# Score rows fetched ten queries at a time into a fixed ring of ten slots, in an attention and gated feed-forward kernel

## The chip, the cores and the metric

The kernel runs on one core of one Trainium2 chip. The metric is the device time of one execution in microseconds (us); lower is better. Time before: 1014.11 us, median of 3 runs (1013.52 to 1015.11).

## What is computed

The inputs are float32: q, k, v of 4 batches x 12 heads x 448 rows x 64, two 12 x 12 matrices w_pre and w_post that mix heads, and the feed-forward weights of 768 x 2048 and 2048 x 768. The reference, cut to what matters:

```python
scores = scale * np.matmul(q, k.transpose(0, 1, 3, 2))
scores = np.einsum('bhij,hg->bgij', scores, w_pre)
scores = scores - np.max(scores, axis=-1, keepdims=True)
attn = np.exp(scores)
attn = attn / (np.sum(attn, axis=-1, keepdims=True) + 1e-09)
attn = np.einsum('bhij,hg->bgij', attn, w_post)
x = np.matmul(attn, v)          # heads side by side: 1792 x 768
h = x @ w_in
g = np.where(h >= 1, h, np.where(h <= -1, 0.0, (h + 1) ** 2 / 4.0))
out = g @ w_out
```

## The kernel before, in words

The program has two stages: attention, up to about 600 us, and the two feed-forward products after it. The change is in the first.

**Tiles and units.** A tile is 120 queries of one batch (the last of a batch has 88); there are 16. `scores` (lines 165 to 174) multiplies Q by K for all heads of a tile and `copy` puts the result into `ssb`, a buffer with the query on the partition and 12 heads x 448 keys along it. Mixing heads needs the heads on the partitions. So a tile is cut into units of 20 queries (the short tile has four and one of 8), and the rows of a unit are fetched from `ssb` into row tiles named `s`: one partition for each pair of query and head. Line 85 lists a unit's queries: two rows of ten queries each, a row's queries `np_` apart (6, in a short tile 4), and `k` = 2 says that a row is cut into two halves of five.

**Fetching** (`load_s`, lines 188 to 196). Each row tile takes two DMAs, one for the five queries of even rank (60 partitions, 0 to 59) and one for those of odd rank (64 to 123). They are issued on SyncE's queue (SP):

```python
for j in range(k):
    a = o + st * j
    nc.sync.dma_start(out=x[64 * j:64 * j + i * H], in_=ssb[t][a:a + st * k * (i - 1) + 1:st * k])
```

The row tiles come from a pool with ten buffers.

**Mixing and softmax.** `pre` (line 206) multiplies each half of a row tile by `wpre`, a block-diagonal matrix of five copies of w_pre, into PSUM (`ps_l`); the four products of a unit go to the four quarters of TensorE. `row_max` (L210, VectorE) finds the maxima, `exps` (L218, ScalarE) the exponentials, `norm` (L225 to L228, GpSimd and VectorE) the scaled copies `wr` of w_post, and `post` (L246) mixes the heads again and turns keys onto the partitions. `pv` (L270) multiplies by V.

**Order.** It is written out by hand: the loop at line 850 goes over 48 steps, each with a group of two units (the last group of a short tile has one). In step n the program places: `load_s` of the units of step n+1; `pre` of step n; `post` of the first unit of step n-1; transposes of a later tile's Q and, in some steps, K (L157, L141); `pv`; `scores` of two pairs of heads of a later tile; `post` of the other unit. In 32 of the steps a chunk of the feed-forward weights is loaded (`wraw`, L302, 768 KB), converted on ScalarE, VectorE and GpSimd, and stored to DRAM (L328, 384 KB); all of these DMAs are on SP's queue, behind `load_s`. Every DMA waits for the eighth DMA before it on that queue, since eight semaphores are used in turn (DMAHW0 to DMAHW7 in the rows of the order).

**Set-up.** GpSimd builds `ident` and one mask, loads the small matrices (L736), and issues four K loads (L738). VectorE makes `wpre` and `wpost` from mask and matrices (L771, L775).

Of the kernel before, what the change touches and what calls it, by code (L numbers as in the profile page):

```python
# [9 lines left out]
F32 = mybir.dt.float32  # L10
# [5 lines left out]
ALU = mybir.AluOpType  # L16
# [6 lines left out]
def tile_talking_heads_moe(  # L23
# [11 lines left out]
    nc = tc.nc  # L35
    B, H, S, D = q.shape
# [4 lines left out]
    IH = 5  # L41
    KH = IH * H
    QT = 24 * IH
    KC = 4
# [13 lines left out]
    ap_ = s_att.enter_context(tc.tile_pool(name="att", bufs=2))  # L58
# [17 lines left out]
    for b in range(B):  # L76
        for i0 in range(0, S, QT):
            t = len(tiles)
            n = min(QT, S - i0)
# [6 lines left out]
            if n > 4 * IH * np_:  # L86
                i = (n - 4 * IH * np_) // 2
# [11 lines left out]
    ssb = {}  # L99
# [6 lines left out]
    def pair(name):  # L106
        return ps_l.tile([128, 2, 512], F32, tag="l", name=name)

    def load_k(b, hp, t=None):
        es = {0: (nc.sync, nc.scalar), 1: (nc.sync, nc.scalar), 4: (nc.gpsimd,) * 2,  # L110
              5: (nc.gpsimd,) * 2}.get(hp if t is not None else None, (nc.sync,) * 2)
        w = 2 * KC * D
        if t is None:
            t = qp.tile([128, w], F32, tag="kraw", name="kraw", bufs=2)
            x = t[:KP]
        else:
            x = t[:KP, w * (hp % 2):w * (hp % 2 + 1)]
        x = x.rearrange("p (r s d) -> p r s d", s=2, d=D)
        for s in range(2):
            es[s].dma_start(out=x[:, :, s, :], in_=k[b, 2 * hp + s].rearrange("(p r) d -> p r d", r=KC))  # L120
        kraw[b, hp] = x

    def load_q(t, gs=(0, 1)):
        b, i0, n, nb = tiles[t]
        if 0 in gs:
            qraw[t] = qp.tile([128, H, D], F32, tag="qraw", name="qraw", bufs=2)
        for g in gs:
            h = slice(g * HP, (g + 1) * HP)
            nc.sync.dma_start(out=qraw[t][:n, h], in_=q[b, h, i0:i0 + n].rearrange("h p d -> p h d"))
# [46 lines left out]
    def copy(e, out, in_):  # L176
        if e is nc.vector:
            nc.vector.tensor_copy(out=out, in_=in_)  # L178
        else:
            nc.scalar.activation(out=out, in_=in_, func=AF.Copy)  # L180

    s10 = {}
    lps = {}
    ex = {}
    wr = {}
    aT = {}

    def load_s(m):
        t, rows, k, c = units[m]
        s10[m] = []  # L190
        for o, st, i in rows:
            x = ap_.tile([128, S], F32, tag="s10", name="s10", bufs=10)
            for j in range(k):
                a = o + st * j
                nc.sync.dma_start(out=x[64 * j:64 * j + i * H], in_=ssb[t][a:a + st * k * (i - 1) + 1:st * k])  # L195
            s10[m].append(x)

    def pre(m):
        t, rows, k, c = units[m]
        ps = lps[m] = pair("ps_l")  # L200
        xs = s10.pop(m)
        n = rows[0][2] * H
        for j in range(k):
            p = slice(64 * j, 64 * j + n)
            for x, h in zip(xs, half):
                nc.tensor.matmul(out=ps[h, j, :S], lhsT=wpre[p], rhs=x[p], start=True, stop=True)  # L206

# [27 lines left out]
    def post(m):  # L235
        t, rows, k, c = units[m]
        if t not in aT:
            aT[t] = ap_.tile([128, KC * H, QT], F32, tag="aT", name="aT")
        n = rows[0][2]
        ps = pair("ps_a")  # L240
        for j, (e, w) in enumerate(zip(ex.pop(m), wr.pop(m))):
            for r in range(KC):
                for x, p in enumerate((slice(0, KH), slice(64, 64 + KH))):
                    o = ps[:, x, :KC * KH * k].rearrange("p (r g i j) -> p r g i j", r=KC, g=H, j=k)
                    for y, h in enumerate((slice(0, 64), slice(64, KP))):
                        nc.tensor.matmul(out=o[h, r, :, :n, j], lhsT=e[p, r * KP + h.start:r * KP + h.stop],  # L246
                                         rhs=w[p].rearrange("p (g i) -> p g i", i=IH)[:, :, :n],
                                         start=True, stop=True)

        def out(e):  # L250
            z = n * k
            copy(e, aT[t][:KP, :, c:c + 2 * z].rearrange("p h (x i) -> p x h i", x=2),
                 ps[:KP, :, :KC * KH * k].rearrange("p x (h i) -> p x h i", h=KC * H)[:, :, :, :z])
        return out
# [450 lines left out]
    with tc.manual_schedule():  # L705
# [6 lines left out]
        ident = qp.tile([128, 128], F32, name="ident", bufs=1)  # L712
# [5 lines left out]
        for hp in (2, 3):  # L718
            load_k(0, hp, k0[1])
        load_q(1)  # L720
        wrep = ap_.tile([128, 4, KH], F32, tag="wr", name="wrep", bufs=2)
        wrep = wrep.rearrange("p a b -> p (a b)")[:, :2 * H].rearrange("p (n h) -> p n h", n=2)
        make_identity(nc, ident)
        nc.gpsimd.memset(wrep, 0.0)
        mask = ap_.tile([128, 4, KH], F32, tag="wr", name="mask", bufs=2)
        mask = mask.rearrange("p a b -> p (a b)")[:, :2 * IH].rearrange("p (n i) -> p n i", n=2)
        nc.gpsimd.memset(mask, 1.0)
        nc.gpsimd.affine_select(out=mask, in_=mask, compare_op=ALU.is_ge, fill=0.0,
                                base=0, pattern=[[-64, 2], [-H, IH]], channel_multiplier=1)
        nc.gpsimd.affine_select(out=mask, in_=mask, compare_op=ALU.is_ge, fill=0.0,  # L730
                                base=H - 1, pattern=[[64, 2], [H, IH]], channel_multiplier=-1)
        nc.gpsimd.tensor_tensor(out=mask[:, 0], in0=mask[:, 0], in1=mask[:, 1], op=ALU.add)
        mask = mask[:, 0]
        for n, w in enumerate((w_pre, w_post)):
            for p in range(2):
                nc.gpsimd.dma_start(out=wrep[64 * p:64 * p + KH, n, :], in_=w.unsqueeze(0).to_broadcast([IH, H, H]))  # L736
        for hp in (4, 5):
            load_k(0, hp, k0[2])  # L738

        ps_w = pair("ps_w")  # L740

# [24 lines left out]
        for m in groups[0]:  # L766
            load_s(m)
# [2 lines left out]
        nc.vector.memset(wpre, 0.0)  # L770
        nc.vector.scalar_tensor_tensor(  # L771
            out=wpre[:, :KH].rearrange("p (i g) -> p i g", g=H),
            in0=mask.unsqueeze(2).to_broadcast([128, IH, H]), scalar=float(D) ** -0.5,
            in1=wrep[:, 0, :].unsqueeze(1).to_broadcast([128, IH, H]), op0=ALU.mult, op1=ALU.mult)
        nc.vector.tensor_tensor(  # L775
            out=wpost.rearrange("p (g i) -> p g i", i=IH),
            in0=wrep[:, 1, :].unsqueeze(2).to_broadcast([128, H, IH]),
            in1=mask.unsqueeze(1).to_broadcast([128, H, IH]), op=ALU.mult)
        for hp in range(4):
            scored_now(1, hp)  # L780
        at = {}
# [68 lines left out]
        for n in range(NG + 2):  # L850
            if n == NE:
# [5 lines left out]
                    name="ps_h", bufs=1, space=PSUM, side="right", reuse_waits="tile"))  # L857
# [5 lines left out]
            if n + 1 < NG:  # L863
                for m in groups[n + 1]:
                    load_s(m)
# [5 lines left out]
            j = 0  # L871
            part = []
            for m in ms:
                pre(m)
                part.append(slice(j, j + units[m][2]))
                j += units[m][2]
            if n == NG:
                step(0)
            posted = [post(old.pop(0))] if old else []
            turned = [f() for f in at.pop(n, ())]  # L880
            for f in mid.pop(n, ()):
# [5 lines left out]
            if old:  # L887
                posted.append(post(old.pop(0)))
# [41 lines left out]
        for j in range(NJ):  # L930
            q, k = divmod(j, 7)
# [143 lines left out]
```

## Time and profile before

| | |
|---|---|
| median of 3 runs | 1014.11 us |
| the profiled execution | 1014.48 us |
| its span, first to last instruction | 1012.8 us |
| mean granted TensorE clock, share of full speed | 0.924 |
| TensorE (PE) busy | 922.1 us |
| VectorE, ScalarE, GpSimd busy | 614.1, 515.8, 108.0 us |
| row tile fetches, number and size | 352 of 105 KB, 8 of 84 KB |

The profile is of one execution, and its page cuts the span into 40 equal slices, so that a digit stands for 25 us. The page's list of costly instructions says for each line how long its engine sat idle just before it and what ended that; the chain follows the work that ended last back to its releasers. Matmuls that run on different quarters overlap, so the mean duration of one, times their number, is more than the busy time.

### The profile page before, as it was taken

What the parts mean: (1) busy time and instruction counts of PE and PEld (TensorE: products, weight loads), DVE (VectorE), ACT (ScalarE), POOL (GpSimd) and SP (SyncE); (2) the same over time, 40 slices, a digit from 0 to 9 for tenths busy, and PEclk for the clock granted to TensorE, in tenths of its full rate; (3) what the DMA queues carried; (4) which work ended last, traced back from release to release, by engine and by line L of the source; (5) the groups of instructions that cost most, each with busy time, mean ns of one, the idle gap of its engine ahead of it and who ended that gap; (6) DMA issues with size and microseconds to landing.
All of it is one profiled execution on the core that took longest, in us unless ns stands there. A gap on an engine that the chain in (4) does not pass through costs nothing.

```text
span 1012.8 us, 25676 instructions
## 1 busy us (share of the span) xinstructions
PE 922.1 (91%) x10986; PEld 716.8 (71%) x10986; DVE 614.1 (61%) x732; ACT 515.8 (51%) x932; POOL 108.0 (11%) x147
## 2 busy tenths in 40 slices
PE   8888898888898897898989689999999999999998
PEld 5455565454565454654656477888999999999998
DVE  4445455445554444554445388879966797867763
ACT  4536454545555445455446345666866754443331
POOL 2012102212112112022122020000000000000000
PEclk9879898889998778899779799999999999999999
DMA  7466566765556665566664637546444445313441
GB/s 148 148 180 175 160 157 176 208 194 160 168 151 188 202 198 160 149 178 197 195 196 153 186 106 244 191 165 230 156 128 135 150 140 176 122 48 95 124 139 57
DMA packets 148946, 162.84 MB, mean 161 GB/s; under 512 B 61132, under 2 KB 142432, under 8 KB 148832
## 3 DMA queue, kind: packets, MB, share of 16 engines
q1 hardware_dynamic: 147584, 160.49, 53.2%
q8 instruction: 87, 1.43, 0.6%
q0 software_dynamic: 320, 0.47, 0.3%
q10 hardware_dynamic: 928, 0.23, 0.1%
q14 instruction: 27, 0.22, 0.1%
HBM read 88.81 MB, written 33.82 MB: 121 GB/s over the span
## 4 chain that ended last, share of the span: by engine, by line
PE 58%; DMA 29%; SPq 7%; ACT 2%; DVE 2%; issue 1%; POOLq 1%; ACTq 0%; DVEq 0%
DMA s<-ssb 21%; PE ps_f L659 20%; PE ps_f L494 20%; PE ps_l L206 5%; PE ps_x L270 5%; PE ps_a L246 4%; SPq L195 4%; PE ps_s L172 3%; DMA wraw<-in_moe_w_out_dram 3%; ACT e L218 1%; DMA v<-in_v_dram 1%; DMA wsd<-wt 1%; DMA wraw<-in_moe_w_in_dram 1%; DMA k<-in_k_dram 1%; DVE nm L210 1%
## 5 line engine op out<-in xcount | busy, mean ns | idle before, releaser
L206 PE MATMUL ps_l<-s,wpre 60*64 60x448 f32 (+1 forms) x720 | 206.1, 598 | 54.3 <-DMA s<-ssb 50.6
L218 ACT ACTIVATE e<-ps_l,nm 128x448 f32<-128x448 f32 x180 | 112.3, 631 | 158.4 <-DVE nm L210 158.3
L206 PEld LDWEIGHTS ps_l<-s,wpre 60*64 60x64 f32 (+1 forms) x720 | 46.7, 137 | 169.4 <-DMA s<-ssb 130.1
L210 DVE TENSOR_REDUCE nm<-ps_l 128x2 f32<-128x896 f32 (+1 forms) x92 | 97.3, 1068 | 97.7 <-PE ps_l L206 97.2
L246 PEld LDWEIGHTS ps_a<-wr,e 60*64 60x64 f32 (+1 forms) x5760 | 122.7, 142 | 44.2 <-issue 30.3
L246 PE MATMUL ps_a<-wr,e 60*64 60x60 f32 (+2 forms) x5760 | 135.2, 237 | 8.8 <-ACT e L218 5.7
L270 PE MATMUL ps_x<-aT,v 112*64 112x120 f32 (+1 forms) x1408 | 98.4, 306 | 4.9 <-DVE kl L146 4.8
L642 ACT ACTIVATE sgh_p<-gq_p 128x1024 fp32r<-128x1024 f32 (+1 forms) x56 | 53.3, 953 | 90.1 <-PE ps_f L659 90.0
L659 PE MATMUL ps_f<-wh,sgh_p 128*128 128x384 f32 x294 | 98.2, 334 | 0.0
L659 PE MATMUL ps_f<-wh,sgl_p 128*128 128x384 f32 x294 | 98.2, 334 | 0.0
L659 PE MATMUL ps_f<-wl,sgh_p 128*128 128x384 f32 x294 | 98.2, 334 | 0.0
L178 DVE COPY ssb<-ps_s 120x896 f32<-120x896 f32 (+1 forms) x48 | 52.3, 1090 | 75.4 <-PE ps_s L172 71.6
L270 PEld LDWEIGHTS ps_x<-aT,v 112*64 112x64 f32 x1408 | 87.6, 166 | 11.8 <-DVE kl L146 6.9
L386 DVE SCALAR_TENSOR_TENSOR wl<-wi,wh 128x768 fp32r<-128x768 f32 x71 | 67.8, 954 | 41.9 <-ACT wh L383 41.9
L383 ACT ACTIVATE wh<-wi 128x768 fp32r<-128x768 f32 x71 | 59.7, 842 | 57.6 <-DVE wi L606 18.0
L643 DVE TENSOR_TENSOR sgl_p<-gq_p,sgh_p 128x1024 fp32r<-128x1024 f32 (+1 forms) x56 | 60.9, 1089 | 33.2 <-ACT sgh_p L642 33.2
L180 ACT ACTIVATE ssb<-ps_s 120x896 f32<-120x896 f32 (+1 forms) x48 | 44.0, 917 | 51.5 <-PE ps_s L172 50.3
L317 POOL TENSOR_TENSOR wt<-wt,wk 128x768 int32<-128x768 int32 x32 | 57.8, 1808 | 100.2 <-ACT wk L316 89.4
L178 DVE COPY aT<-ps_a 112x960 f32<-112x960 f32 x48 | 55.3, 1152 | 8.6 <-PE ps_a L246 8.5
L322 DVE TENSOR_SCALAR wt<-wt 128x768 int32<-128x768 int32 x32 | 17.9, 560 | 68.8 <-ACT wt L310 68.8
L659 PEld LDWEIGHTS ps_f<-wl,sgh_p 128*128 128x128 f32 x294 | 55.2, 188 | 0.0
L659 PEld LDWEIGHTS ps_f<-wh,sgh_p 128*128 128x128 f32 x294 | 55.2, 188 | 0.0
(209 smaller groups left out, 1661.3 us busy)
## 6 DMA issues: line engine op xcount, KB each, us to landing
s<-ssb SPq DMA_DIRECT2D x352, 105.0 KB
wraw<-in_moe_w_in_dram SPq DMA_DIRECT2D x16, 768.0 KB
wraw<-in_moe_w_out_dram SPq DMA_DIRECT2D x16, 768.0 KB
wi<-wod SPq DMA_DIRECT2D x29, 384.0 KB
wi<-wsd SPq DMA_DIRECT2D x28, 384.0 KB
wsd<-wt SPq DMA_DIRECT2D x16, 384.0 KB
wod<-wt SPq DMA_DIRECT2D x16, 384.0 KB
wi<-wss SPq DMA_DIRECT2D x16, 384.0 KB
```

Of the source, the lines that this page charges most:

```text
L178: nc.vector.tensor_copy(out=out, in_=in_)
L206: nc.tensor.matmul(out=ps[h, j, :S], lhsT=wpre[p], rhs=x[p], start=True, stop=True)
L210: nc.vector.tensor_reduce(out=nm, in_=lps[m][:, :k, :S], axis=AX.X, op=ALU.max, negate=True)
L218: nc.scalar.activation(out=e, in_=ps[:, j, :S], func=AF.Exp, bias=nm[:, j:j + 1], accum_out=sm[:, j:j + 1])
L246: nc.tensor.matmul(out=o[h, r, :, :n, j], lhsT=e[p, r * KP + h.start:r * KP + h.stop], rhs=w[p].rearrange("p (g i) -> p g i", i=IH)[:, :, :n],
L270: nc.tensor.matmul(out=ps[half[s], m, :n], lhsT=vt[b, g][:, 2 * m + s, r * D:(r + 1) * D], rhs=a[:KP, r * H + h, :n], start=(r == 0), stop ...
L317: nc.gpsimd.tensor_tensor(out=t, in0=t, in1=k, op=ALU.add)
L383: nc.scalar.activation(out=hi, in_=t, func=AF.Copy, scale=2.0 ** -8)
L386: nc.vector.scalar_tensor_tensor(out=lo, in0=t, scalar=2.0 ** -8, in1=hi.bitcast(F32), op0=ALU.mult, op1=ALU.subtract)
L494: nc.tensor.matmul(out=o, lhsT=u[:, c, k], rhs=x, start=first and r == 0 and m == 0, stop=r == 2 and m == 2, skip_group_check=True)
L643: nc.vector.tensor_tensor(out=lo, in0=src, in1=hi.bitcast(F32), op=ALU.subtract)
L659: nc.tensor.matmul(out=o, lhsT=x[:, f, c], rhs=y[:, f % 2, :], start=first and f == 0 and m == 0, stop=hf == 1 and f == 3 and m == 2, skip ...
```

## The change

`load_s` fetches a row tile with one DMA: ten queries, 120 partitions, from partition 4 to 123. The destination is a slot of one fixed tile, `srows`, of ten slots, taken in turn, in place of ten pool buffers. Partitions 0 to 3 of all slots are set to zero once, by GpSimd. The lower half of a row tile now begins at partition 4, and its product contracts partitions 0 to 63 (four of them zero); the upper half is 64 to 123 as before. The first five queries of a row are in the lower half and the last five in the upper one, where they were even and odd ranks; `post` therefore writes its PSUM columns with the half outside the query (`j i` for `i j`). `wpre` is built with a second mask, shifted by four partitions, and its small matrix comes with one DMA for 120 partitions.

```diff
+    R0 = 4
+    NS = 10
+    srow = [0]
...
         for o, st, i in rows:
-            x = ap_.tile([128, S], F32, tag="s10", name="s10", bufs=10)
-            for j in range(k):
-                a = o + st * j
-                nc.sync.dma_start(out=x[64 * j:64 * j + i * H], in_=ssb[t][a:a + st * k * (i - 1) + 1:st * k])
+            x = srows[:, srow[0] % NS]
+            srow[0] += 1
+            i *= k
+            nc.sync.dma_start(out=x[R0:R0 + i * H], in_=ssb[t][o:o + st * (i - 1) + 1:st])
             s10[m].append(x)
...
-            p = slice(64 * j, 64 * j + n)
+            p = slice(64 * j, 64 if k == 2 and j == 0 else R0 + 60 * j + n)
             for x, h in zip(xs, half):
                 nc.tensor.matmul(out=ps[h, j, :S], lhsT=wpre[p], rhs=x[p], start=True, stop=True)
...
-                    o = ps[:, x, :KC * KH * k].rearrange("p (r g i j) -> p r g i j", r=KC, g=H, j=k)
+                    o = ps[:, x, :KC * KH * k].rearrange("p (r g j i) -> p r g i j", r=KC, g=H, j=k)
...
+        srows = ap_.tile([128, NS, S], F32, name="srows", bufs=1)
+        make_identity(nc, ident)
...
-        make_identity(nc, ident)
         nc.gpsimd.memset(wrep, 0.0)
...
+        masks = ap_.tile([128, 4, KH], F32, tag="wr", name="mask", bufs=2)
+        masks = masks.rearrange("p a b -> p (a b)")[:, :4 * IH].rearrange("p (m n i) -> p m n i", m=2, n=2)
+        nc.gpsimd.memset(masks, 1.0)
+        for m in range(2):
+            x = masks[:, m]
+            w = (KH, 64)[m]
+            nc.gpsimd.affine_select(out=x, in_=x, compare_op=ALU.is_ge, fill=0.0,
+                                    base=(-R0, 0)[m], pattern=[[-w, 2], [-H, IH]], channel_multiplier=1)
+            nc.gpsimd.affine_select(out=x, in_=x, compare_op=ALU.is_ge, fill=0.0,
+                                    base=(R0, 0)[m] + H - 1, pattern=[[w, 2], [H, IH]], channel_multiplier=-1)
...
+        nc.gpsimd.dma_start(out=wrep[R0:R0 + 2 * KH, 0, :], in_=w_pre.unsqueeze(0).to_broadcast([2 * IH, H, H]))
+        for p in range(2):
+            nc.gpsimd.dma_start(out=wrep[64 * p:64 * p + KH, 1, :], in_=w_post.unsqueeze(0).to_broadcast([IH, H, H]))
         for hp in (4, 5):
             load_k(0, hp, k0[2])
+        nc.gpsimd.memset(srows[:R0], 0.0)
```

On SP's queue the order of the DMAs stays, with one fetch where two stood. A row shows line, operation, output and input, shape, and the semaphores waited for. This is the part of the queue before the change for the fetches of step 5 and the weight chunk behind them:

```order
L195 DMA s_641<-ssb 60x1x448 [waits DMAHW4_49,PE_49]
L195 DMA s_641<-ssb 60x1x448 [waits DMAHW5_49]
L195 DMA s_644<-ssb 60x1x448 [waits DMAHW6_49,PE_49]
L195 DMA s_644<-ssb 60x1x448 [waits DMAHW7_49]
L195 DMA s_647<-ssb 60x1x448 [waits DMAHW0_49,PE_49]
L195 DMA s_647<-ssb 60x1x448 [waits DMAHW1_49]
L195 DMA s_650<-ssb 60x1x448 [waits DMAHW2_49,PE_49]
L195 DMA s_650<-ssb 60x1x448 [waits DMAHW3_49]
L302 DMA wraw<-in_moe_w_in_dram 128x6x128 [waits DMAHW4_49,DVE_49,Activation_49]
L328 DMA wsd<-wt 128x2x384 [waits DMAHW5_49,Pool_49]
```

And the same place after it (the lines of the kernel have moved by three):

```order
L198 DMA srows<-ssb 120x1x448 [waits DMAHW4_49,PE_49]
L198 DMA srows<-ssb 120x1x448 [waits DMAHW5_49,PE_49]
L198 DMA srows<-ssb 120x1x448 [waits DMAHW6_49,PE_49]
L198 DMA srows<-ssb 120x1x448 [waits DMAHW7_49,PE_49]
L305 DMA wraw<-in_moe_w_in_dram 128x6x128 [waits DMAHW0_49,DVE_49,Activation_49]
L331 DMA wsd<-wt 128x2x384 [waits DMAHW1_49,Pool_49]
```

Eight fetches have become four; the ring of ten slots still makes each wait for TensorE's use of the slot ten fetches earlier, and the eighth DMA before a fetch now lies about a step back.

On TensorE the first products of step 2, before:

```order
L206 MATMUL ps_l<-s_379,wpre 64x448 [waits DMAHW7_49,DVE_49,Activation_49]
L206 MATMUL ps_l<-s_382,wpre 64x448 [waits DMAHW1_49]
L206 MATMUL ps_l<-s_379,wpre 64x448 [waits DMAHW0_49]
L206 MATMUL ps_l<-s_382,wpre 64x448 [waits DMAHW2_49]
L206 MATMUL ps_l<-s_385,wpre 64x448 [waits DMAHW3_49,DVE_49]
L206 MATMUL ps_l<-s_388,wpre 64x448 [waits DMAHW5_49]
L206 MATMUL ps_l<-s_385,wpre 64x448 [waits DMAHW4_49]
L206 MATMUL ps_l<-s_388,wpre 64x448 [waits DMAHW6_49]
```

And after:

```order
L209 MATMUL ps_l<-srows,wpre 64x448 [waits DMAHW7_49,DVE_49,Activation_49]
L209 MATMUL ps_l<-srows,wpre 64x448 [waits DMAHW0_49]
L209 MATMUL ps_l<-srows,wpre 64x448 x2
L209 MATMUL ps_l<-srows,wpre 64x448 [waits DMAHW1_49,DVE_49]
L209 MATMUL ps_l<-srows,wpre 64x448 [waits DMAHW2_49]
L209 MATMUL ps_l<-srows,wpre 64x448 x2
```

The eight products stay where they were; a wait for a fetch now covers both halves of a row tile, so two of each four products wait for none of their own.

## Rows read from the trace of the kernel before

**Rows 1.** The page, sections 1 and 2: busy time; slices of clock and DMA share.

```profile
PE 922.1 (91%) x10986; PEld 716.8 (71%) x10986; DVE 614.1 (61%) x732; ACT 515.8 (51%) x932; POOL 108.0 (11%) x147
...
PEclk9879898889998778899779799999999999999999
DMA  7466566765556665566664637546444445313441
```

**Rows 2.** The page, section 4: the chain that ended last, by engine and line.

```profile
PE 58%; DMA 29%; SPq 7%; ACT 2%; DVE 2%; issue 1%; POOLq 1%; ACTq 0%; DVEq 0%
DMA s<-ssb 21%; PE ps_f L659 20%; PE ps_f L494 20%; PE ps_l L206 5%; PE ps_x L270 5%; PE ps_a L246 4%; SPq L195 4%; PE ps_s L172 3%; DMA wraw<-in_moe_w_out_dram 3%; ACT e L218 1%; DMA v<-in_v_dram 1%; DMA wsd<-wt 1%; DMA wraw<-in_moe_w_in_dram 1%; DMA k<-in_k_dram 1%; DVE nm L210 1%
```

**Rows 3.** Stages (start:end, length, busy us of each engine, clock, DMA share, GB/s).

```profile
20.00:600.00 580.00, 497.84 (x8621) 318.90 (x8623) 287.13 (x363) 290.05 (x624) 101.21 (x128) 0.87 0.60 173
620.00:1013.00 393.00, 387.41 (x2097) 368.84 (x2095) 299.23 (x329) 202.96 (x267) 0.00 (x0) 1.00 0.44 141
```

**Rows 4.** Waits of PE, 20 to 600 us: us, times, longest us.

```profile
PE ps_l L206 <- DMA s<-ssb: 50.6, 61, 2.2
PE ps_t L157 <- DVE kl L146: 12.2, 6, 2.8
PE ps_a L246 <- ACT e L218: 5.7, 1, 5.7
```

**Rows 5.** Five whole steps, columns as in rows 3.

```profile
354.63:372.54 17.91, 15.48 (x200) 9.48 (x195) 6.38 (x8) 6.73 (x15) 2.90 (x4) 0.71 0.72 199
372.54:381.69 9.15, 8.66 (x209) 5.81 (x199) 6.13 (x8) 6.96 (x16) 2.20 (x3) 1.00 0.58 191
317.98:327.64 9.66, 8.45 (x192) 5.53 (x192) 7.06 (x10) 6.59 (x15) 2.70 (x4) 1.00 0.54 178
...
78.71:87.85 9.14, 8.77 (x207) 5.87 (x197) 6.12 (x8) 6.74 (x16) 2.03 (x2) 1.00 0.46 151
502.97:516.27 13.30, 11.46 (x200) 6.79 (x194) 6.38 (x8) 6.72 (x15) 2.52 (x4) 0.87 0.66 198
```

**Rows 6.** Products of `pre`: count, duration ns min/median/max, first and last start us.

```profile
L206 PE MATMUL ps_l<-s,wpre x720: 533/542/1006, 21.0 to 584.2; 60*64 60x448 f32 x176, 48*64 48x448 f32 x4
```

**Rows 7.** Stretches before and after the clock falls, columns as in rows 3.

```profile
385.10:388.50 3.40, 1.25 (x14) 0.49 (x18) 0.59 (x1) 1.34 (x4) 1.53 (x1) 1.00 0.68 210
388.50:395.30 6.80, 6.80 (x102) 5.66 (x97) 2.25 (x2) 1.71 (x5) 0.22 (x1) 0.50 0.38 126
518.20:521.60 3.40, 1.82 (x12) 0.60 (x16) 2.52 (x3) 1.57 (x4) 1.53 (x1) 1.00 0.92 264
521.60:528.40 6.80, 6.80 (x103) 5.66 (x98) 2.68 (x3) 2.34 (x9) 0.50 (x2) 0.50 0.46 137
```

**Rows 8.** The page, section 6: fetches, number and size of one.

```profile
s<-ssb SPq DMA_DIRECT2D x352, 105.0 KB
```

**Rows 9.** Stretches where nearly only fetches move, columns as in rows 3.

```profile
22.50:25.00 2.50, 2.10 (x6) 0.38 (x4) 1.09 (x1) 0.17 (x1) 0.00 (x0) 1.00 0.32 113
...
555.50:557.00 1.50, 1.50 (x15) 0.63 (x12) 0.00 (x0) 0.70 (x2) 0.59 (x1) 1.00 0.31 115
564.60:566.00 1.40, 1.40 (x20) 0.53 (x16) 0.10 (x1) 0.84 (x2) 0.59 (x1) 1.00 0.23 24
```

**Rows 10.** Issues of fetches on SP's queue (all; the two of 48 rows).

```profile
L195 SPq DMA_DIRECT2D s<-ssb x360: 652/742/3189, 17.1 to 576.2; - x180
...
L195 SPq DMA_DIRECT2D s<-ssb x2: 670/682/693, 562.0 to 562.8; - x2
```

**Rows 11.** Products of `post`: a unit of 8 queries, and one of 20.

```profile
L246 PE MATMUL ps_a<-wr,e x32: 205/218/253, 302.8 to 303.3; 60*64 60x48 f32 x16, 60*48 60x48 f32 x16
...
L246 PE MATMUL ps_a<-wr,e x52: 212/216/263, 322.6 to 323.4; 60*48 60x60 f32 x28, 60*64 60x60 f32 x24
```

**Rows 12.** GpSimd at the start: start us, us, instruction.

```profile
0.79 0.20 POOL masks.py:197 MEMSET ident<- 128x128 f32 x1 [0.29 <-POOLq L1059]
...
4.79 2.88 POOL L120 DMA_DIRECT2D k<-in_k_dram  x4
```

More of the change, by code (lines that the diff above doesn't have):

```diff
@@ L720, in tile_talking_heads_moe @@
         load_q(1)
+        srows = ap_.tile([128, NS, S], F32, name="srows", bufs=1)
+        make_identity(nc, ident)
         wrep = ap_.tile([128, 4, KH], F32, tag="wr", name="wrep", bufs=2)
         wrep = wrep.rearrange("p a b -> p (a b)")[:, :2 * H].rearrange("p (n h) -> p n h", n=2)
-        make_identity(nc, ident)
         nc.gpsimd.memset(wrep, 0.0)
-        mask = ap_.tile([128, 4, KH], F32, tag="wr", name="mask", bufs=2)
-        mask = mask.rearrange("p a b -> p (a b)")[:, :2 * IH].rearrange("p (n i) -> p n i", n=2)
@@ L727, in tile_talking_heads_moe @@
[L727 to L733, printed above, removed]
@@ L734, in tile_talking_heads_moe @@
-        for n, w in enumerate((w_pre, w_post)):
-            for p in range(2):
-                nc.gpsimd.dma_start(out=wrep[64 * p:64 * p + KH, n, :], in_=w.unsqueeze(0).to_broadcast([IH, H, H]))
+        masks = ap_.tile([128, 4, KH], F32, tag="wr", name="mask", bufs=2)
[8 more added lines that the diff above has]
+                                    base=(R0, 0)[m] + H - 1, pattern=[[w, 2], [H, IH]], channel_multiplier=-1)
@@ L737, in tile_talking_heads_moe @@
+        nc.gpsimd.tensor_tensor(out=masks[:, :, 0], in0=masks[:, :, 0], in1=masks[:, :, 1], op=ALU.add)
+        mask = [masks[:, m, 0] for m in range(2)]
+        nc.gpsimd.dma_start(out=wrep[R0:R0 + 2 * KH, 0, :], in_=w_pre.unsqueeze(0).to_broadcast([2 * IH, H, H]))
+        for p in range(2):
+            nc.gpsimd.dma_start(out=wrep[64 * p:64 * p + KH, 1, :], in_=w_post.unsqueeze(0).to_broadcast([IH, H, H]))
         for hp in (4, 5):
             load_k(0, hp, k0[2])
+        nc.gpsimd.memset(srows[:R0], 0.0)
@@ L772, in tile_talking_heads_moe @@
             out=wpre[:, :KH].rearrange("p (i g) -> p i g", g=H),
-            in0=mask.unsqueeze(2).to_broadcast([128, IH, H]), scalar=float(D) ** -0.5,
+            in0=mask[0].unsqueeze(2).to_broadcast([128, IH, H]), scalar=float(D) ** -0.5,
             in1=wrep[:, 0, :].unsqueeze(1).to_broadcast([128, IH, H]), op0=ALU.mult, op1=ALU.mult)
@@ L777, in tile_talking_heads_moe @@
             in0=wrep[:, 1, :].unsqueeze(2).to_broadcast([128, H, IH]),
-            in1=mask.unsqueeze(1).to_broadcast([128, H, IH]), op=ALU.mult)
+            in1=mask[1].unsqueeze(1).to_broadcast([128, H, IH]), op=ALU.mult)
         for hp in range(4):
```

## The prediction, made before the changed kernel was run

> **What bounds the kernel now.** I read the page's head first. TensorE is busy 91% of the span, but the slices of its clock stay at full speed only from slice 25 on; in the 24 before it, attention, they stand between 7 and 9 [rows 1]. So the second stage has nothing to give, and attention has. The chain names what: 21% of the span is the fetch of score rows, `s<-ssb`, the largest entry [rows 2].
>
> The table by stage puts numbers on it [rows 3]: from 20 to 600 us TensorE is busy 498 of 580 us at a mean clock of 0.87, VectorE and ScalarE half the time. The list of waits says who ends TensorE's idle time there [rows 4]: the fetch 61 times, 50.6 us; the next cause has 12.2 us.
>
> The single steps show what a wait really costs [rows 5]. Steps with next to no such wait take 9.15, 9.66 and 9.14 us at clock 1.00. Steps with waits take 17.91 and 13.30 us, at clock 0.71 and 0.87. The work is the same; the wait is only 1 to 2.5 us of it, and the rest is the clock. [Rows 7] show the link: in the stretch before a fall TensorE was busy 1.25 of 3.40 and 1.82 of 3.40 us, then the clock is 0.50 and TensorE is busy 6.80 of 6.80 us, doing half as much. The two levels are 2.4 and 1.2 GHz.
>
> Why the fetch is late: 352 fetches of 105 KB (107,520 bytes) are 37.8 MB [rows 8], and the eight of 84 KB make it 38.5 MB. Where almost nothing but fetches moves, the rate is 113 and 115 GB/s at a share of 0.32 and 0.31 of 16 engines, which is five engines [rows 9]: as many as a fetch has queries. In the last of these rows the fetches of four queries run, and the share is 0.23, about four. At 115 GB/s all fetches take 335 us of those five. The mean share of 0.60 of 580 us is 348 us for each engine [rows 3]; the fetches are 335 x 5/16 = 105 of that, so other traffic is 243 us on every engine, if it is spread evenly. The five engines then carry 335 + 243 = 578 of 580 us. They are the bound, and the other eleven are not.
>
> **The change, part by part.**
>
> *Fetches on ten engines.* A fetch now has ten queries. If the count of engines follows the count of queries, as five and four do [rows 9], ten engines each move twelve rows, as each of five does now: a fetch of twice the size takes the same time, and there are half as many. Fetch time on an engine falls from 335 to 167 us, the load of the busiest engines from 578 to 167 + 243 = 410 us. No row shows a fetch on ten engines. Its bounds are 167 us and, if it stays on five, the 335 us of now; I take 167, which is where the two counts seen point. The Trainium skill, "DMA: Bandwidth & Descriptors", section "Why a DMA increments its semaphore by 16 and not by 1", gives ten here, the largest number up to 16 that divides both 10 and 120.
>
> *TensorE's waits.* Its own work is the next bound. Mean clock 0.87 means 26% of 580 us, 151 us, at half speed, with TensorE busy nearly throughout [rows 3, 7]; at full speed that is 75 us less, so about 422 us of work. Transfers at 410 us are just below it and are issued a step ahead, but not evenly, so I leave 8 of the 50.6 us [rows 4]: **-43 us**.
>
> *The clock.* At stake are the 75 us. Falls that follow other waits stay (17.9 us in the two others of [rows 4], among them the steps that transpose K). I take three fifths back: **-45 us**. The ends are 0 and 75.
>
> *SP's queue.* Issues fall from 360 to 184. One takes 742 ns, of 48 rows 682 ns [rows 10]: 5 ns a row, so a fetch of 120 rows would take about 1.04 us; the ends are 0.74 and 1.48 us. Even 1.48 is what two cost now, so the queue loses nothing; at 1.04 us it gains 176 x 0.44 = 77 us, all beside TensorE's work and already in the waits above. Each DMA waits for the eighth before it; with four fetches fewer in a step, that one is older. Behind a fetch stand the weight chunks and their stores, which come no later.
>
> *Products.* `pre` contracts 64 rows for 60 in the lower half. Rows of 48 and 60 lie together at a median of 542 ns with a least of 533 [rows 6]; zero, at most 9 ns x 360 products that overlap by four, 1 us. `post` writes 12 runs of five. The nearest is the unit of eight queries, which writes 12 runs of four: 218 ns against 216 [rows 11]. Zero, and at most 2 ns x 5632 = 11 us.
>
> *Set-up.* GpSimd's new memset is 4480 elements long; at the 0.20 us for 128 of the nearest row it takes 7 us at most, after the K loads that begin at 4.79 and take 2.88 us [rows 12]. It ends by about 15 us, and the first product is at 21.0 us [rows 6]: zero, covered by the first fetch. Were the cover gone, it would be those 7 us, once. A mask more and a small load less ahead of the K loads cancel to a few tenths.
>
> **Sum.** 1012.8 - 43 - 45 = 924.8 us of span, and 1.7 us around it: 926.5 us for the execution profiled. That execution is 0.4 us above the median, so **926 us**. A check: `pre` runs from 21.0 to 584.2 us [rows 6], 48 steps, about 12.0 us each. All at 9.3 us, the mean of the three free ones [rows 5], would give 47 x 2.7 = 127 us, 888 us in all. I expect some seven tenths of it.
>
> **The rivals.**
>
> *Rows that share a way out of memory (0.12).* Ten sources 6 apart hold pairs 30 to 34 apart, which could stand in each other's way. Four neighbouring sources together got 24 GB/s [rows 9], what one engine gets alone (115/5 = 23), so sharing is real here. If pairs near 32 apart shared too, in two thirds of the fetches engines 1, 3, 6 and 8 would take twice as long: 8 x 2 + 4 = 20 units for a tile's twelve fetches, where a tile now costs 24. Busiest engines: 335 x 20/24 + 243 = 522 of 578, so 580 x 522/578 = 524, a gain of 56: **about 958 us**. Against it: from 555.5 us the fetches had sources 8 apart, the first and the last exactly 32 apart, and moved 115 GB/s, no less than the 113 GB/s at the start, where none are [rows 9]. The Trainium skill, "SBUF — State Buffer", section "Door 1: The DMA port swizzle", says that partitions 32 apart in a half use the same port; by that rule this rival would be the forecast. The trace shows the sharing for neighbours and not for 32 apart.
>
> *The queue or the rest takes over (0.13).* If an issue costs 1.48 us or more, or if weight chunks and stores crowd the ten engines, half of both terms stays: **about 970 us**. For it: SP holds 7% of the chain [rows 2], and 410 against 422 us is close. Against it: free steps exist with chunk loads beside them [rows 5].
>
> *Slower: a fetch stays on five engines (0.04).* Then the change does not do what it says. The load stays 578 us, but a fetch of 120 rows takes twice as long to land, and a product that began after 60 rows waits for 120. At each of the 61 waits [rows 4] one more product of 0.54 us [rows 6] comes after the last landing, up to 33 us, half of it likely: **about 1030 us**. It decides if the share of DMA beside fetches alone stays at 0.31. Against it: four queries gave less than five [rows 9].
>
> *No change (0.02):* another wait takes all. *Below 900 us (0.07):* waits and falls go nearly together. The forecast, 900 to 950 us, has 0.62.
>
> **Range and chances.** The low end, 893 us, is near the check with nothing left over; the high end, 970, takes in the first two rivals and half of both terms. Outside lie the slower case, no change and the tails. A measurement of this kernel tells 0.2% from no change, about 2 us: faster 0.94, within it 0.02, slower 0.04.
>
> **What would show it.** Right: where only fetches move, a DMA share near 0.62 and some 230 GB/s; TensorE's waits for the fetch under 15 us; a clock above 0.92 from the start of attention to its end; a typical step of 9 to 10 us; an issue near 1 us. A share of 0.31 beside fetches is the slower rival; 0.62 at much less than 230 GB/s is the shared rows; waits of SP or of the weight conversion in the place of the fetch are the second rival. The forecast is wrong if the waits go and the clock does not follow: then 970 us, by the first term alone.

## The result, and the profile of the changed kernel

The changed kernel takes **907.7 us** (median of 4 runs, 901.72 to 918.59) against 1014.2 us for the kernel before on the same chip: a ratio of 0.893, 95% interval 0.8881 to 0.8978. The forecast was 926 us, with a range of 893 to 970. Ratios in this document leave out runs that were slower at a lower granted clock, here the one of 918.59 us. The profiled execution took 905.92 us, with a span of 904.2 us, 108.6 us less than before.

First the page of the changed kernel, sections 1 and 2, which answers to [rows 1]; a digit now stands for 22.6 us:

```profile
PE 819.0 (91%) x10986; PEld 673.8 (75%) x10986; DVE 610.1 (67%) x732; ACT 512.8 (57%) x932; POOL 111.8 (12%) x149
...
PEclk9989898999999989998999999999999999999999
DMA  8788559986679976798673763764444454214341
```

TensorE's share is 91% as before, but the 7s of its clock are gone, and the DMA engines are fuller during attention: the same traffic in less time. Next its chain, section 4, beside [rows 2]:

```profile
PE 58%; DMA 20%; ACT 8%; DVE 7%; issue 3%; SPq 3%; POOLq 1%; POOL 0%; ACTq 0%; DVEq 0%
PE ps_f L662 23%; PE ps_f L497 20%; DMA srows<-ssb 12%; PE ps_x L273 4%; ACT e L221 4%; PE ps_s L172 4%; PE ps_a L249 3%; PE ps_l L209 3%; DVE nm L213 2%; DMA wod<-wt 2%; DMA wraw<-in_moe_w_in_dram 2%; ACT wt L313 1%; SPq L198 1%; DVE wt L326 1%; DMA k<-in_k_dram 1%
```

The fetch fell from 21% to 12%; ScalarE and VectorE came up from 2% each to 8% and 7%. By stage (columns as in [rows 3]; attention first, then the rest):

```profile
20.00:490.00 470.00, 394.31 (x8612) 274.79 (x8612) 282.67 (x362) 287.52 (x623) 101.37 (x128) 0.94 0.77 214
491.00:904.00 413.00, 407.73 (x2266) 385.92 (x2264) 316.67 (x352) 216.39 (x294) 0.00 (x0) 1.00 0.45 143
```

The second stage has the length it had: 413 us from 600 us to the end before, 413 us from 491 us now. Attention went from 580 to 470 us, and these rows split the difference into three parts. A mean clock of 0.94 means 12% of 470 us at half speed, 56 us, which costs 28 us; before, the same sum gave 75 us. So the **clock gave 47 us**. Idle time is length less busy time: 75.7 us now, 82.2 us before, so **idle time gave only 6.5 us**. What is left is busy time at full speed: 394 - 28 = 366 us against the 422 of the prediction, so **TensorE's "work" fell by 56 us**, though it does the same products. The list of waits says why the idle time hardly moved (changed kernel, PE, 20 to 490 us; us, times, longest us; beside [rows 4]):

```profile
PE ps_l L209 <- DMA srows<-ssb: 18.7, 36, 1.6
PE ps_t L157 <- DVE kl L146: 17.4, 6, 4.8
PE ps_s L172 <- ACT e L221: 7.4, 14, 1.7
PE ps_x L273 <- DVE kl L146: 6.0, 3, 2.0
PE ps_a L249 <- issue: 5.6, 6, 2.2
...
PE ps_l L209 <- DVE ssb L178: 4.5, 7, 0.8
```

The fetch lost 32 of 50.6 us, and other causes took most of it: transposes of Q that wait behind K (12.2 to 17.4 us), scores that wait for the exponentials (7.4 us, 0.5 before), products that wait for the next tile's scores.

For the 56 us, see how long a group of products lasts. Before, at the start of the step at 354.63 us of [rows 5], the timeline of PE has (start us, us, instructions, idle before them):

```profile
354.63 3.12 PE L206 MATMUL ps_l<-s,wpre 60*64 60x448 f32 x8
358.14 0.93 PE L206 MATMUL ps_l<-s,wpre 60*64 60x448 f32 x2 [0.39 <-DMA s<-ssb]
```

The trace has two instructions for each product (sixteen where the order of step 2 has eight), so the first row is the four products of one unit. They took 3.12 us at full clock, and the first product of the next unit took 0.93. The table of stretches for these 3.12 us (columns as in [rows 3]) has TensorE busy in nearly all of them:

```profile
354.63:357.75 3.12, 2.85 (x18) 0.52 (x10) 1.04 (x2) 2.62 (x4) 0.44 (x1) 1.00 0.85 222
```

The products were not computing all that time. In the trace they start at 354.63, 355.67, 355.68 and 356.79 us, as their fetches land, and TensorE counts as busy while any one of them runs. The waiting was inside the busy time. The page's groups show it whole, first before and then after (count | busy us, mean ns | idle us before them):

```profile
L206 PE MATMUL ps_l<-s,wpre 60*64 60x448 f32 (+1 forms) x720 | 206.1, 598 | 54.3 <-DMA s<-ssb 50.6
```

```profile
L209 PE MATMUL ps_l<-srows,wpre 64*64 64x448 f32 (+2 forms) x720 | 126.7, 591 | 24.1 <-DMA srows<-ssb 18.7
```

The same 720 instructions, at nearly the same mean, hold TensorE for 126.7 in place of 206.1 us.

Single steps of the changed kernel (columns as in [rows 3], beside [rows 5]):

```profile
196.50:205.57 9.07, 8.74 (x198) 5.49 (x191) 5.75 (x7) 6.31 (x14) 2.63 (x4) 1.00 0.90 267
85.11:100.42 15.31, 10.46 (x215) 8.15 (x208) 6.82 (x8) 7.36 (x16) 2.55 (x3) 0.78 0.53 156
```

Most are like the first. The second is one of three long ones, of 14.5 to 15.4 us, in which K is transposed. Its timeline on PE and on DVE shows the wait:

```profile
87.74 0.99 PE L141 MATMUL ps_k<-ident,kraw 112*128 112x112 f32 x8
93.58 0.86 PE L157 MATMUL ps_t<-ident,qraw 120*128 120x120 f32 x3 [4.85 <-DVE kl L146]
```

```profile
87.86 0.96 DVE L326 SCALAR_TENSOR_TENSOR wt<-wraw,wt 128x768 int32<-128x768 int32 x1
88.74 2.08 DVE L213 TENSOR_REDUCE nm<-ps_l 128x2 f32<-128x896 f32 x2
90.74 1.15 DVE L178 COPY aT<-ps_a 112x960 f32<-112x960 f32 x1
92.90 1.15 DVE L146 TENSOR_TENSOR kl<-ps_k,kh 128x448 fp32r<-128x448 f32 x2 [1.01 <-ACT kh L145]
```

TensorE waits 4.85 us for `kl`. VectorE is not too busy for it: it sits idle for 1.01 us just before, until ScalarE has made `kh`. ScalarE's timeline has the rest:

```profile
87.14 0.93 ACT L319 ACTIVATE wk<-wraw 128x768 int32<-128x768 uint32 x1
89.86 0.63 ACT L221 ACTIVATE e<-ps_l,nm 128x448 f32<-128x448 f32 x1 [1.79 <-DVE nm L213]
...
92.31 0.99 ACT L145 ACTIVATE kh<-ps_k 128x448 fp32r<-128x448 f32 x2
```

TensorE has finished the transposes of K (`ps_k`) by 88.73 us, but `kh` stands on ScalarE behind the exponentials, and these wait for VectorE's maxima, which stand behind a weight conversion. With the products ahead of it done sooner, TensorE arrives here earlier than the two engines do.

### The profile page after: what moved, and what is told of

Its sections match the earlier page's. It is cut to its first block, busy times and chain, and to the rows that moved or that the text cites. A ratio compares the mean times of both kernels' runs of the same rounds, so it can differ in the third digit from the quotient of the medians.

```text
span 904.2 us, 25499 instructions
## 1 busy us (share of the span) xinstructions
PE 819.0 (91%) x10986; PEld 673.8 (75%) x10986; DVE 610.1 (67%) x732; ACT 512.8 (57%) x932; POOL 111.8 (12%) x149
## 4 chain that ended last, share of the span: by engine, by line
PE 58%; DMA 20%; ACT 8%; DVE 7%; issue 3%; SPq 3%; POOLq 1%; POOL 0%; ACTq 0%; DVEq 0%
PE ps_f L662 23%; PE ps_f L497 20%; DMA srows<-ssb 12%; PE ps_x L273 4%; ACT e L221 4%; PE ps_s L172 4%; PE ps_a L249 3%; PE ps_l L209 3%; DVE nm L213 2%; DMA wod<-wt 2%; DMA wraw<-in_moe_w_in_dram 2%; ACT wt L313 1%; SPq L198 1%; DVE wt L326 1%; DMA k<-in_k_dram 1%
## 5 line engine op out<-in xcount | busy, mean ns | idle before, releaser
L209 PE MATMUL ps_l<-srows,wpre 64*64 64x448 f32 (+2 forms) x720 | 126.7, 591 | 24.1 <-DMA srows<-ssb 18.7
L249 PEld LDWEIGHTS ps_a<-wr,e 60*64 60x64 f32 (+1 forms) x5760 | 110.0, 132 | 49.0 <-issue 29.7
L249 PE MATMUL ps_a<-wr,e 60*48 60x60 f32 (+2 forms) x5760 | 120.3, 223 | 14.0 <-issue 5.6
L213 DVE TENSOR_REDUCE nm<-ps_l 128x2 f32<-128x896 f32 (+1 forms) x92 | 95.3, 1065 | 26.3 <-PE ps_l L209 26.1
L209 PEld LDWEIGHTS ps_l<-srows,wpre 64*64 64x64 f32 (+2 forms) x720 | 34.0, 138 | 80.5 <-DMA srows<-ssb 34.0
L273 PE MATMUL ps_x<-aT,v 112*64 112x120 f32 (+1 forms) x1408 | 83.2, 274 | 9.0 <-DVE kl L146 6.0
L273 PEld LDWEIGHTS ps_x<-aT,v 112*64 112x64 f32 x1408 | 73.6, 145 | 15.1 <-DVE kl L146 8.2
```

Of the source, the lines that this page charges most:

```text
L213: nc.vector.tensor_reduce(out=nm, in_=lps[m][:, :k, :S], axis=AX.X, op=ALU.max, negate=True)
L273: nc.tensor.matmul(out=ps[half[s], m, :n], lhsT=vt[b, g][:, 2 * m + s, r * D:(r + 1) * D], rhs=a[:KP, r * H + h, :n], start=(r == 0), stop ...
```

## The experiments

Ten kernels ran, two of them twice. Unless said otherwise each edit is on the changed kernel, and ratios are to the kernel before on the same chip, with 95% intervals. Where an expectation names a theory A, it is the prediction's: the time follows the number of engines that carry a fetch. Its rivals are that the number of issues on SP's queue decides, and that the ring, with its other waits, does.

### Two fetches of five queries, in the new ring

```diff
-            nc.sync.dma_start(out=x[R0:R0 + i * H], in_=ssb[t][o:o + st * (i - 1) + 1:st])
+            for j in range(k):
+                w, a, p = i // k, o + st * (i // k) * j, R0 + 60 * j
+                nc.sync.dma_start(out=x[p:p + w * H], in_=ssb[t][a:a + st * (w - 1) + 1:st])
```

> The changed kernel, ring, masks and order of columns included, but each row tile fetched again by two transfers of five queries each (360 fetches). Theory A, the number of DMA engines behind a fetch is what counts: five engines carry 335 + 243 us again, so 1000 to 1020 us, a DMA share of 0.31 beside fetches, TensorE's waits for the fetch near 50 us. Theory B, the gain is in the ring, the layout or the products: below 940 us.

Measured: 1002.01 us, 0.9873 [0.984, 0.9906]. The stretch from 22 to 30 us, where mostly fetches move, in this kernel and then in the changed one (columns as in [rows 3]):

```profile
22.00:30.00 8.00, 6.29 (x28) 1.96 (x26) 3.02 (x3) 2.69 (x8) 0.00 (x0) 1.00 0.32 119
```

```profile
22.00:30.00 8.00, 6.35 (x41) 2.24 (x42) 3.64 (x5) 4.11 (x10) 0.65 (x2) 1.00 0.58 182
```

A share of 0.32 of 16 is five engines, and 0.58 is about nine. The ring, the 64-row products and the set-up of the change are all in this kernel, and nearly all of the gain is gone.

### The same with half the keys

As the one above, but only keys 0 to 223 are fetched; the rest of a row tile is zero.

```diff
-                nc.sync.dma_start(out=x[p:p + w * H], in_=ssb[t][a:a + st * (w - 1) + 1:st])
+                nc.sync.dma_start(out=x[p:p + w * H, :S // 2], in_=ssb[t][a:a + st * (w - 1) + 1:st, :, :S // 2])
...
-        nc.gpsimd.memset(srows[:R0], 0.0)
+        nc.gpsimd.memset(srows, 0.0)
```

> Two transfers of five queries again, 360 fetches as before, but only keys 0 to 223 of each row are fetched; the rest of a row tile stays at the zeros of one memset, so half of the scores is left out. Theory A, transfer time on the five engines: their load falls to 335/2 + 243 = 410 us, the same as with ten engines, so 905 to 935 us. Theory C, the number of issues on SP's queue and of the waits that come with them: those are as before, so 990 to 1020 us.

Measured: 901.03 us, 0.8875 [0.8834, 0.8917]. Five engines with half the bytes, in 360 issues, are as fast as ten engines with all of them in 184. That is a little under theory A's 905 to 935 us and far from theory C's. In both a busy engine carries the same bytes of scores. So it is the load of the busiest engines that set the time, and not, in the main, the number of issues. The time in which a row tile lands goes with that load in both kernels, and no run parts the two.

### More issues

A second, tiny transfer of 4 x 12 numbers, into four partitions that nothing reads, behind each fetch of the first 14 tiles: 156 issues more.

```diff
+            if k == 2 and t < len(tiles) - 2:
+                w = H * ((srow[0] - 1) // NS)
+                nc.sync.dma_start(out=x[124:, w:w + H], in_=ssb[t][o:o + st * 3 + 1:st, :, :1])
```

> The changed kernel with a small transfer of 4 x 12 elements of 4 bytes, which nobody reads, issued behind each fetch of the first 14 tiles: 156 issues more, so about as many as before, in the same places of the queue, and ten engines behind each fetch. Theory A: SP's queue gets some 110 us more of issues beside TensorE's work, the time stays under 935 us. Theory C: back to 980 to 1015 us.

Measured: 925.12 us, 0.9095 [0.9044, 0.9145]. Issues are not free: 156 of them cost some 17 us, but most of the gain stays. TensorE's waits for the fetch did not grow (14.8 us, 20 times).

### Ten engines, half the keys

```diff
-            nc.sync.dma_start(out=x[R0:R0 + i * H], in_=ssb[t][o:o + st * (i - 1) + 1:st])
+            nc.sync.dma_start(out=x[R0:R0 + i * H, :S // 2], in_=ssb[t][o:o + st * (i - 1) + 1:st, :, :S // 2])
...
-        nc.gpsimd.memset(srows[:R0], 0.0)
+        nc.gpsimd.memset(srows, 0.0)
```

> The changed kernel with only keys 0 to 223 fetched (the other half of the scores is left out, zeros stand there): what transfers still cost after the change. Theory A with the ten engines still near their limit: the waits of TensorE for the fetch, 18.7 us after the change, fall under 5 us, the stretches at half clock behind them go, 885 to 897 us. Rival: other waits than the fetch set the pace now, and nothing moves beyond 5 us, 903 to 912 us.

Measured: 866.05 us, 0.855 [0.8505, 0.8595], some 20 us below what was expected. Its group on the page, and a group of products in its timeline:

```profile
L209 PE MATMUL ps_l<-srows,wpre 64*64 64x448 f32 (+2 forms) x720 | 82.7, 548 | 8.7 <-DVE ssb L178 8.6
...
246.63 1.74 PE L209 MATMUL ps_l<-srows,wpre 64*64 64x448 f32 x16
```

Sixteen instructions, the products of two units, take 1.74 us when nothing is late, and all 720 hold TensorE for 82.7 us. The expectation missed by the term that the prediction had missed: the 18.7 us of idle time were counted, but not the 126.7 - 82.7 = 44 us that still lay inside the busy time. Against these 82.7 us the kernel before had 123 us more there, waiting for the most part and in part half clock. The transfers still cost some 40 us after the change.

### What else was in the change: even and odd ranks, and the ring alone

Two fetches went back to even and odd ranks in the new ring; and, on the kernel before, only the pool was replaced by the ring.

```diff
-            nc.sync.dma_start(out=x[R0:R0 + i * H], in_=ssb[t][o:o + st * (i - 1) + 1:st])
+            w = i // k
+            for j in range(k):
+                a, p = o + st * j, R0 + 60 * j
+                nc.sync.dma_start(out=x[p:p + w * H], in_=ssb[t][a:a + st * k * (w - 1) + 1:st * k])
...
-                    o = ps[:, x, :KC * KH * k].rearrange("p (r g j i) -> p r g i j", r=KC, g=H, j=k)
+                    o = ps[:, x, :KC * KH * k].rearrange("p (r g i j) -> p r g i j", r=KC, g=H, j=k)
```

> Two transfers of five queries into the fixed ring, the queries of even and of odd rank apart as in the kernel before (sources 12 apart, columns of the product as there); what is left of the change is the ring, the four zero rows and the second mask. The kernel with two transfers of neighbouring ranks took 1002.0 us, 12 less than before. Theory D, those 12 us come from the order of queries (sources 6 apart, runs of five in the product): 1010 to 1018 us here. Theory E, they come from the ring and its waits: 998 to 1006 us.

```diff
+    srow = [0]
...
-            x = ap_.tile([128, S], F32, tag="s10", name="s10", bufs=10)
+            x = srows[:, srow[0] % 10]
+            srow[0] += 1
...
+        srows = ap_.tile([128, 10, S], F32, name="srows", bufs=1)
```

> The kernel before with one edit: the row tiles are slots of one fixed tile, taken in turn, in place of ten pool buffers; the two fetches of five queries, their partitions (0 to 59 and 64 to 123) and the products of 60 rows are as before. two_even_odd, which has the new partitions and the 64-row products too, took 0.9916 of the time before. If those 8 us are the ring's, 1003 to 1010 us here; if they are those of the new partitions or of the mask and small loads at the start, 1011 to 1018 us.

Measured: 1006.3 us, 0.9916 [0.9889, 0.9944], and 1007.39 us, 0.9926 [0.9898, 0.9955]. The first lies at the edge of theory E's range, the second inside the ring's. The ring alone is worth some 7 to 8 us, and new partitions, 64-row products and set-up add nothing that can be told from it. Nor can the order of queries be told: the interval of the first overlaps that of the two fetches of neighbouring ranks (0.984 to 0.9906). How the ring gains its part stays open. Waits of TensorE for the fetch are no shorter with it (52.1 us, 70 times, against [rows 4]); in the execution profiled the clock of attention is higher:

```profile
20.00:594.00 574.00, 489.37 (x8655) 311.64 (x8656) 287.24 (x364) 290.99 (x626) 100.97 (x128) 0.89 0.60 175
```

### Where the sources lie

In a tile of 120 queries the ten sources of a fetch lie 6 partitions apart, so some pairs are 30 apart. In the first of these kernels the two row tiles of a unit take queries in turn, and sources are 12 apart. In the second they are neighbours.

```diff
-                units.append((t, [(o + np_ * 2 * IH * r, np_, IH) for r in range(2)], 2, 4 * IH * o))
+                rows = [(o + np_ * r, 2 * np_, IH) if n == QT else (o + np_ * 2 * IH * r, np_, IH) for r in range(2)]
+                units.append((t, rows, 2, 4 * IH * o))
...
+            order = "p h (i x) -> p x h i" if k == 2 and tiles[t][2] == QT else "p h (x i) -> p x h i"
```

> The changed kernel, but in tiles of 120 queries the two row tiles of a unit take turns, so that the ten sources of a fetch are 12 partitions apart and none stands 32 (or 28 to 35) from another in the same half; the copy behind the second mixing puts the columns back in order. Theory F, pairs of sources near 32 apart hold each other up: fetches land faster, TensorE's waits for them fall from 18.7 us to under 12, 893 to 903 us. Rival, they do not: 904 to 912 us, or a little more for the copies that now write with a step of two.

```diff
-            nc.sync.dma_start(out=x[R0:R0 + i * H], in_=ssb[t][o:o + st * (i - 1) + 1:st])
+            a, d = o, st
+            if k == 2:
+                a, d = 20 * (c // 20) + 10 * len(s10[m]), 1
+            nc.sync.dma_start(out=x[R0:R0 + i * H], in_=ssb[t][a:a + d * (i - 1) + 1:d])
```

> The changed kernel, but a fetch takes ten neighbouring queries (sources 1 apart; the queries of a unit are other ones, so the rows of the result land in other places). In the kernel before, four neighbouring sources together got 24 GB/s, what one gets alone. Theory F for neighbours: four of ten engines share one way, a fetch takes some 3.2 us in place of 0.9, 176 of them 563 us, with 243 us of other traffic 806 us for the busiest engines: 1130 to 1260 us. Rival, ten engines hide it: under 960 us.

Measured: 905.61 us, 0.8919 [0.887, 0.8968], and 1011.08 us in a single run, which falls in neither theory's range. The stretch from 22 to 30 us in each:

```profile
22.00:30.00 8.00, 7.48 (x106) 3.40 (x108) 5.54 (x7) 4.69 (x11) 0.81 (x2) 1.00 0.64 232
```

```profile
22.00:30.00 8.00, 4.86 (x13) 1.07 (x16) 1.09 (x1) 1.46 (x4) 0.00 (x0) 0.59 0.53 101
```

In this bunch of fetches, sources 12 apart move 232 GB/s where those 6 apart move 182, and neighbours move 101. So sources do hold each other up, neighbours so much that the whole gain is lost. But 232 for 182 GB/s changed nothing in the time. It did change what TensorE waits for. With sources 12 apart, its waits (20 to 480 us) and its group of products are (this execution was the slowest of four, 912.69 us):

```profile
PE ps_t L158 <- DVE kl L147: 20.7, 6, 4.9
PE ps_s L173 <- ACT e L222: 14.0, 19, 1.7
PE ps_l L210 <- DMA srows<-ssb: 13.7, 23, 2.3
...
L210 PE MATMUL ps_l<-srows,wpre 64*64 64x448 f32 (+2 forms) x720 | 109.2, 574 | 20.5 <-DMA srows<-ssb 13.7
```

The waits for the fetch fell from 18.7 to 13.7 us, less far than theory F asked, and the products hold TensorE for 109.2 us in place of 126.7. But the waits for the exponentials rose from 7.4 to 14.0 us and those for `kl` from 17.4 to 20.7: what the fetch gave back, waits for ScalarE and VectorE took.

### The steps that transpose K

In the nine steps that transpose K, the scores now stand ahead of the transposes of Q that wait for `kl`, and the copies follow that order.

```diff
+            fs = list(at.pop(n, ()))
+            ksteps = len(fs) > 1
-            turned = [f() for f in at.pop(n, ())]
+            turned = [f() for f in (fs[:2] if ksteps else fs)]
...
+            scored = [scores(*x) for x in vis.pop(n, ())] if ksteps else None
+            turned += [f() for f in fs[2:]] if ksteps else []
             copies = [pv(*x, n) for x in vis2.pop(n, ())] if early else []
-            scored = [scores(*x) for x in vis.pop(n, ())]
+            if scored is None:
+                scored = [scores(*x) for x in vis.pop(n, ())]
...
-            for f in copies:
-                f()
+            if not ksteps:
+                for f in copies:
+                    f()
...
+            if ksteps:
+                for f in copies:
+                    f()
```

> The changed kernel; in the nine steps that transpose K, TensorE does the products of scores ahead of the transposes of Q and of the product with V, and the copies follow that order. Theory G, the waits of the transposes for VectorE's copies (17.4 us, L157 behind L146) and the half clock behind them are the next bound: 885 to 898 us. Rival, the waits only move to the next instruction that needs those copies: 903 to 912 us.

> k_steps_later once more, on the same chip as the next one: 888 to 896 us.

Measured: 891.28 us, 0.8739 [0.8682, 0.8796], and again 885.37 us, 0.8731 [0.8709, 0.8754]; both intervals lie below that of the change, and the second median lies 3 us under the 888 to 896 us expected of it. PE's waits, and SP's, in the second of them (20 to 480 us):

```profile
PE ps_t L157 <- DVE kl L146: 3.0, 6, 0.8
...
SPq L198 <- DVE ssb L178: 15.1, 8, 4.1
```

The wait for `kl` fell from 17.4 to 3.0 us. On SP's queue the fetches that wait for the scores to be copied fell too; in the changed kernel that row stands at

```profile
SPq L198 <- DVE ssb L178: 41.3, 10, 8.2
```

This version beats both kernels.

### Both

> The changed kernel with both edits that were made apart: the K-transposing steps in the order of k_steps_later, and the sources of a fetch twelve apart as in sources_12_apart. If the faster landing is again worth nothing, 886 to 897 us, the time of k_steps_later (891.3). If with the K-transposing steps out of the way the fetches are what TensorE waits for next, their faster landing counts, and it takes 875 to 886 us.

> k_steps_and_12_apart once more. If the sources twelve apart are worth something here, its interval lies below that of k_steps_later_2, by 5 to 10 us in the medians; if the 8 us between the two earlier runs were the spread of such runs, within 3 us of it.

Measured: 882.99 us, 0.869 [0.8659, 0.8722], and again 886.4 us, 0.8717 [0.8683, 0.875]. The first fell into the band that was to mean that sources 12 apart count. Run on one chip beside the other version, nothing of that is left: 886.4 against 885.4 us, with intervals that overlap. So the 8 us between the first two results are best read as the spread of such runs.

## Why the prediction was right, and where it was not

**Ten engines: right.** The share beside fetches is 0.58 (0.62 forecast), and the two runs with half the keys show that the load of the busiest engines decides. The Trainium skill, "DMA: Bandwidth & Descriptors", section "Why a DMA increments its semaphore by 16 and not by 1", gives the count as the largest number up to 16 that divides the slowest dimension of the source and that of the destination; shares of 0.32 with five queries and 0.58 to 0.64 with ten agree. The 230 GB/s came only with sources 12 apart; the changed kernel has 182.

**TensorE's waits, -43 us: the step that failed.** It left 8 us of waiting for the fetch; 18.7 stayed, and other waits took most of what went, so idle time fell by 6.5 us. The rest of the failure is in "about 422 us of work", which was taken as fixed: 56 us of it was waiting that the trace counts as busy, and it went. Both errors are in one term, and together they give -62 us for the -43 forecast. The sum thus came out 20 us above the profiled span (924.8 against 904.2). That the sum came so near is in part luck: the idle time that the term was made of gave 6.5 us, and what made up for it stood in no term.

The median of 542 ns in [rows 6] hid this, as it is the time of one instruction; 720 of them, four at a time, would be 97 us, an estimate that is still too high (82.7 us with half the keys), and the page's 206.1 us of busy time was the sign that wasn't read. The steps of [rows 5] had it too. At full speed the busy time of the two slow ones is 15.48 - 0.29 x 17.91 = 10.3 us and 11.46 - 0.13 x 13.30 = 9.7 us, against 8.45 to 8.77 us in the free ones. So "the rest is the clock" was not the whole of it.

**The clock, -45 us: right**, 47 us. Of the 28 us that stayed, a part is where the prediction put it, in the steps that transpose K (the second of the steps above, at 0.78). The mean of attention is 0.94, over the 0.92 that was asked for, though single slices of the page still show an 8.

**SP's queue: right in kind.** The issue of a fetch, changed kernel (ns min/median/max):

```profile
L198 SPq DMA_DIRECT2D srows<-ssb x184: 659/809/3142, 17.8 to 466.7; - x184
```

0.81 us in place of the 1.04 estimated from 5 ns a row, and inside the ends. That the gain lies beside TensorE's work holds in part: 156 more issues cost 17 us.

**Products: zero, right.** Least and median with 64 rows are no more than those of [rows 6], and `post` with 12 runs of five takes 213 ns, against [rows 11]'s 216 (the second row is a stretch of it):

```profile
L209 PE MATMUL ps_l<-srows,wpre x720: 532/536/1007, 21.8 to 475.8; 64*64 64x448 f32 x139, 60*64 60x448 f32 x37, 52*64 52x448 f32 x4
...
L249 PE MATMUL ps_a<-wr,e x48: 212/213/243, 298.8 to 299.5; 60*48 60x60 f32 x25, 60*64 60x60 f32 x23
```

**Set-up: right.** The memset took 3.82 us and ended at 11.4 us, ahead of the first fetch, which is issued at 17.8 us, 0.7 us later than before:

```profile
7.54 3.82 POOL L746 MEMSET srows<- 4x4480 f32 x1
```

**The rivals.** *Rows that share a way out of memory* was dismissed with the wrong reason. The row at 555.5 us had only its first and last sources 32 apart, and five engines; with ten engines and six apart the sharing is there, 182 against 232 GB/s. The Trainium skill, "SBUF — State Buffer", section "Door 1: The DMA port swizzle", says that partitions 32 apart in a half use one port, and so do the four of a group; by that some pairs 30 apart share one as well, and this pair of rates agrees. Yet its 958 us didn't come, and landing faster was worth nothing in two comparisons: it did shorten the waits for the fetch, and waits for ScalarE and VectorE grew in their place. *The queue or the rest takes over* is there in small, with those waits. *Slower: a fetch stays on five engines* is out by the share of 0.58. *Below 900 us* was nearly the result, but not for the reason given with it: the clock gave back 47 of 75 us, the three fifths of the forecast, and what brought the time down further was the waiting inside the busy time.

## What to carry to other kernels

A product that runs on a quarter of the array counts as busy while its neighbours wait for their data, so check a group's busy time against a stretch in which nothing is late: before the change four products took 3.12 us in one place, and with half the keys eight take 1.74 us. The difference is waiting that no list of waits shows. When transfers are the bound, ask first how many engines one transfer uses, and then which engine carries most bytes. When a wait shrinks, look at the next queue that the same engine meets: here TensorE came earlier to a result that ScalarE and VectorE still made at the same time, and reordering that step gave another 2%.

## What was not expected of the hardware

- Twice the rows on ten engines cost the queue little: 0.81 us an issue for 120 rows, against 0.74 us for 60 on five engines.
- Sources in neighbouring partitions move 101 GB/s at a share of 0.53, those 6 apart 182 GB/s at 0.58. A DMA share alone doesn't tell how much is moved.
- Idle time of TensorE in attention hardly fell (82.2 to 75.7 us), and yet the time at half clock fell to about a third (151 to 56 us). What in the work the clock answers to, the idle time listed or the waiting inside the busy time, no run here told apart.
